# Memory V turned by transposing DMA instead of by the TensorE, at new places, with a branch hint for the sync engine

## The chip, the cores and the metric

The kernel runs on one NeuronCore of a Trainium2 chip. The metric is the device time of one execution in microseconds (us); the tables give the median of all runs of a kernel. "Granted clock" is the share of its full clock that the TensorE was allowed, as the profile gives it.

## The reference, cut to what matters

Two layers are computed side by side and concatenated. A is a complex diagonal recurrence over 2048 steps. B is attention in 64 segments of 32 tokens, each with 8 memory rows in front; the memory of the next segment is the output of the first 8 rows of this one.

```python
def _B_ref(x, mem0, Wq, Wk, Wv, Wo, seg_len):        # 32 heads of 128, model width 1024
    ...
    for s in range(n_seg):
        xs = x[:, s * seg_len:(s + 1) * seg_len, :].copy()
        h = jnp.concatenate([mem, xs], axis=1)
        q, k, v = (jnp.einsum('btd,dhe->bhte', h, W) for W in (Wq, Wk, Wv))   # three lines in the original
        scores = jnp.einsum('bhqe,bhke->bhqk', q, k) * scale
        ...
        o = jnp.einsum('bhqk,bhke->bhqe', softmax(scores), v)                 # two lines in the original
        o = jnp.einsum('bhte,hed->btd', o, Wo)
        mem = o[:, :M, :].copy()
        outs.append(o[:, M:, :])
```

What matters here is V of the 73 memory rows (`NM` = 7 + 66). It is made on the TensorE in eight blocks of four heads ("blocks 0 to 7"), comes out with the head dimension on the partitions, and must be turned so that the rows are on the partitions.

## The kernel before: the parts that the change touches

The kernel has four phases: projections of x, the recurrence (second phase, to about 471 us), the attention by head pairs `hp` = 0 to 15 (third phase), and the output projection. A scheduler orders the instructions of each engine, so program order is only a starting point, except where the code asks for it to be kept.

```python
def stage_init(self):                        # two staging buffers, used in turn
    self.vst = []
    for i in range(2):
        self.vst.append(self.wl.tile([128, 4, 4, EW], BF16, name=f"b_vst{i}", bufs=1))
        self.k.G.memset(self.vst[i][:, :, :, E:EW], 1.0)      # columns of ones, E = 128, EW = 136
    self.nst = 0

def next_st(self):
    self.nst += 1
    return self.vst[self.nst % 2]

def v_mem(self, hb, w=None):                 # block hb of memory V
    k = self.k
    w = w or self.load_wv(hb)
    p = k.ps("P")
    for h in range(4):
        for c in range(KC):
            k.PE.matmul(p[:, h * NM:(h + 1) * NM], w[:, c, h * 128:(h + 1) * 128], self.memT[:, c, :], ...)
    vm = self.vmp.tile([128, 4, NM], BF16, name="b_vm", bufs=1)
    k.copy("v", vm[:], p[:, 0:4 * NM].rearrange("p (h n) -> p h n", h=4))
    yield
    pt = k.ps("P", (128, 1024), BF16)
    for h in range(4):
        k.PE.transpose(pt[0:NM, h * 128:(h + 1) * 128], vm[:, h, :], k.ident[:])
    st = self.next_st()
    k.copy("v", st[0:NM, 0, :, 0:E], pt[0:NM, 0:512].rearrange("p (h e) -> p h e", h=4))
    sv = st[:, 0, :, :].rearrange("p h e -> p (h e)")
    k.SP.dma_start(self.vx[hb][64:64 + NMX, :], sv[0:NMX, :])      # 7 rows
    k.SP.dma_start(self.vt[hb][:], sv[NMX:NM, :])                  # 66 rows
    yield
...
def load_v(self, hp):                        # V of a head pair, for the attention
    vt = self.vts[hp % 2]
    if hp < 2:                               # fill rows 99 to 127 once in each of two buffers: 29 rows
        z = self.vx[0][T + 32:T + 32 + 128 - GW, 0:2 * EW].unsqueeze(1).to_broadcast([128 - GW, NG, 2 * EW])
        k.tc.keep_in_program_order(k.SP.dma_start(vt[GW:128, :, :], z))
    ...                                      # 96 rows from vx, 3 rows from vt
...
def hint(k):                                 # the branch over the rarely needed general path, near the end
    k.tc.mark_branch_hint_location("general", "LikelyTaken", engines=[mybir.EngineType.PE])
    i = k.nc.cur_bb.bb.instructions[-1]
    k.tc.keep_in_program_order(type("Ins", (), {"ins": i}))
...
# second phase, 30 steps i of the recurrence
    if i in (26, 28):
        vm = b.v_mem((i - 26) // 2, wv[(i - 26) // 2])
    if 26 <= i < 30:
        next(vm)
...
# third phase, 11 steps u of each head pair hp
    if n == 12:
        k.SP.dma_start(wo0[:], b.Wo[:, :, 0:512])              # 4 MB
    if hp % 2 == 0 and 2 < hp + 2 < HP:
        if u == 4:
            vm = b.v_mem(hp // 2 + 1)
        if u in (4, 6):
            next(vm)
```

SyncE issues nearly all DMAs (371 of 452 in the trace before), one after the other; a DMA that has to wait holds up those behind it (before, the load of `b_v` from `b_vx` at 466.40 us held SyncE for 16.05 us, and the load behind it went out at 482.50). A DMA has "landed" when its data have arrived and its semaphore says so.

## Time and profile before

| | before |
|---|---|
| median of 3 runs | 1246.7 us (1246.66 to 1246.81) |
| profiled span, granted clock | 1245.3 us, 0.999 |
| TensorE (PE) busy | 1234.2 us, 99% |
| last matmul ends, then to the end of the span | 1239.3 us, 6.0 us |

The page of the kernel before, its first, second and fourth part. In the second part every digit is the busy share, or the granted clock, of one fortieth of the span in tenths. In all views PE is the TensorE, PEld its loads of weights, DVE the VectorE, ACT the ScalarE, POOL the GpSimd engine, SP or SPq the SyncE; names that begin with ps are tiles in PSUM, the memory that the TensorE writes to.

```profile
span 1245.3 us, 20124 instructions
PE 1234.2 (99%) x8270; PEld 662.5 (53%) x8342; DVE 667.7 (54%) x1250; ACT 263.4 (21%) x631; POOL 275.8 (22%) x407
PE   9999999999999999999999999999999999999998
PEclk9999999999999999999999999999999999999999
PE 99%; issue 0%; DVE 0%
```

The TensorE is the bound everywhere. The list of waits of the TensorE over the whole run (engine, line, releaser: total us, times, longest) has one line, at the very start:

```profile
PE psR L64 <- DVE hpb L105: 1.3, 1, 1.3
```

The list of waits of SyncE's queue in the last 45 us shows, beside waits for the data of output stores, one long wait of its own after the closing branch (line L1156):

```profile
SPq L1156 <- SPq L1156: 2.8, 1, 2.8
```

SyncE's timeline around the first V load (start, us taken, engine, operation, out<-in). The V stores take 0.3 us each, and the loads of V follow directly. The last line holds two DMAs: issuing the 29 filler rows takes 0.32 us, and the 96 rows behind them hold SyncE for 16.05 us.

```profile
465.02 0.27 SPq L64 DMA_DIRECT2D b_vx<-b_vst  x1
465.34 0.29 SPq L64 DMA_DIRECT2D b_vt<-b_vst  x1
465.73 0.26 SPq L64 DMA_DIRECT2D b_v<-b_vt  x1
466.03 16.42 SPq L64 DMA_DIRECT2D b_v<-b_vx  x2
```

### The profile page before, as it was taken

The page shows a single profiled execution, that of the slowest core. Times are in us where ns is not written, and L with a number is a line of the kernel's source. Part 1 is how long each engine was busy: PE and PEld are TensorE (multiplying, and loading weights), DVE is VectorE, ACT ScalarE, POOL GpSimd, SP SyncE. Part 2 cuts the span into 40 slices and gives each one's busy share as a digit, 9 for nine tenths or more (in the row PEclk, how much of TensorE's full clock was granted, in tenths as well). Part 3 has the DMA queues.
Part 4 walks back from the last instruction along what each step waited for, and adds up shares of the span by engine and source line. Part 5 has one row for each costly group of instructions (what it writes and reads, how often), then busy time and mean ns, then how long its engine had stood idle before and what let it go on. Part 6 is the DMA issues. An engine that isn't in the chain of part 4 may idle for free.

```text
span 1245.3 us, 20124 instructions
## 1 busy us (share of the span) xinstructions
PE 1234.2 (99%) x8270; PEld 662.5 (53%) x8342; DVE 667.7 (54%) x1250; ACT 263.4 (21%) x631; POOL 275.8 (22%) x407
## 2 busy tenths in 40 slices
PE   9999999999999999999999999999999999999998
PEld 5444444444455555556666656555665554446444
DVE  4688899998711124666666666666666641001000
ACT  5344444443310000211112111111211110000000
POOL 4111331212332321322222222222222220000000
PEclk9999999999999999999999999999999999999999
DMA  9965444554898734664454545545553379407000
GB/s 248 272 191 147 131 135 127 144 155 107 242 322 248 249 116 95 196 170 124 96 145 108 144 108 120 132 92 121 120 142 92 65 211 230 107 18 153 17 26 19
DMA packets 316246, 176.83 MB, mean 142 GB/s; under 512 B 138874, under 2 KB 301550, under 8 KB 316150
## 3 DMA queue, kind: packets, MB, share of 16 engines
q1 hardware_dynamic: 294054, 147.95, 47.8%
q10 hardware_dynamic: 21072, 24.38, 5.9%
q0 software_dynamic: 1024, 3.17, 0.7%
q8 instruction: 66, 1.08, 0.4%
q14 instruction: 30, 0.25, 0.1%
HBM read 89.14 MB, written 53.17 MB: 114 GB/s over the span
## 4 chain that ended last, share of the span: by engine, by line
PE 99%; issue 0%; DVE 0%
PE psP L64 82%; PE psU L64 9%; PE psS L64 3%; PE psO L64 2%; PE psR L64 2%; DVE b_xe L91 0%; DVE b_ost L91 0%; DVE a_n L962 0%; DVE hpb L105 0%; DVE ones L102 0%
## 5 line engine op out<-in xcount | busy, mean ns | idle before, releaser
L64 PE MATMUL psP<-b_xe,b_wq 128*128 128x480 bf16 (+1 forms) x1280 | 247.7, 343 | 0.1
L64 PE MATMUL psP<-b_xe,b_wk 128*128 128x480 bf16 (+1 forms) x1280 | 247.7, 343 | 0.0
L64 PE MATMUL psP<-b_wv,b_xe 128*128 128x512 bf16 (+2 forms) x1033 | 223.4, 372 | 0.8
L644 POOL TENSOR_TENSOR b_m<-b_e,maskB 99x396 bf16<-99x396 bf16 x160 | 139.8, 874 | 338.5 <-ACT b_e L641 338.5
L641 ACT ACTIVATE b_e<-psS 99x396 bf16<-99x396 f32 x176 | 88.2, 501 | 536.7 <-PE psS L64 533.4
L64 PEld LDWEIGHTS <-b_wk 128*128 128x128 bf16 x1280 | 119.4, 98 | 94.2
L64 PEld LDWEIGHTS <-b_wq 128*128 128x128 bf16 x1280 | 118.7, 98 | 87.7
L64 PEld LDWEIGHTS <-b_xe 128*128 128x128 bf16 x1056 | 101.8, 98 | 119.1 <-DVE b_xe L91 0.2
L91 DVE CAST b_k<-psP 128x480 bf16<-128x480 f32 (+1 forms) x192 | 97.4, 528 | 100.9 <-PE psP L64 100.9
L91 DVE CAST b_q<-psP 128x480 bf16<-128x480 f32 (+1 forms) x192 | 97.4, 528 | 93.1 <-PE psP L64 91.5
L64 PEld LDWEIGHTS <-b_ol 128*128 128x128 bf16 x864 | 84.3, 98 | 94.4
L64 PE MATMUL psU<-a_xT,a_bt 128*128 128x512 bf16 x493 | 113.9, 379 | 1.1
L64 PE MATMUL psP<-t,a_hl 128*128 128x512 bf16 x496 | 112.1, 379 | 0.8
L91 DVE CAST b_ost<-psP 128x512 bf16<-128x512 f32 (+1 forms) x17 | 11.5, 676 | 177.4 <-PE psP L64 176.3
L64 PE MATMUL psP<-wo,b_ol 128*128 128x512 bf16 (+1 forms) x440 | 91.9, 364 | 0.4
L64 PE MATMUL psP<-t,b_ol 128*128 128x512 bf16 x408 | 91.7, 379 | 0.4
L280 POOL TENSOR_SCALAR a_tt<-a_pr,a_tabf 128x1 f32<-128x1 f32 x48 | 34.1, 710 | 243.2 <-DVE a_pr L275 243.2
L661 DVE TENSOR_TENSOR b_ob<-psO,b_accR 99x384 bf16<-99x384 f32 x160 | 85.9, 553 | 2.4 <-DVE b_accR L660 0.4
L89 ACT ACTIVATE b_vst<-psP 128x512 bf16<-128x512 f32 x126 | 71.9, 589 | 71.3 <-PE psP L64 59.9
L267 DVE TENSOR_TENSOR a_pr<-psU,a_tabf 128x2048 f32<-128x2048 f32 x32 | 73.0, 2282 | 15.7 <-PE psU L64 14.0
L64 PEld LDWEIGHTS <-a_bt 128*128 128x128 bf16 x512 | 49.2, 98 | 57.6
L64 PEld LDWEIGHTS <-a_hl 128*128 128x128 bf16 x512 | 49.0, 98 | 56.7
(200 smaller groups left out, 962.7 us busy)
## 6 DMA issues: line engine op xcount, KB each, us to landing
b_v<-b_vx SPq DMA_DIRECT2D x16, 1122.0 KB
b_wv<-in_B_Wv_dram SPq DMA_DIRECT2D x16, 1024.0 KB
b_vx<-b_vst ACTq DMA_DIRECT2D x24, 544.0 KB
b_on<-b_ob SPq DMA_DIRECT2D x15, 720.0 KB
a_hs<-a_h SPq DMA_DIRECT2D x32, 256.0 KB
b_wog<-in_B_Wo_dram SPq DMA_DIRECT2D x4, 2048.0 KB
b_wq<-in_B_Wq_dram SPq DMA_DIRECT2D x16, 512.0 KB
b_wk<-in_B_Wk_dram SPq DMA_DIRECT2D x16, 512.0 KB
```

Of the source, the lines that this page charges most:

```text
L64: r = f(*a, **kw)
L89: self.S.activation(out, in_, ACT.Copy)
L91: self.V.tensor_copy(out, in_)
L267: V.tensor_tensor(pr[:], u[:].unsqueeze(1).to_broadcast([128, 2, 2, TB]), view(t3, [[TB + 1, 2], [TB + 1, 2], [1, TB]]), ALU.mult)
L280: G.tensor_scalar(tt[:, j:j + 1], w[:, j, TB - 1:TB], t3[:, 1, TB:TB + 1], None, ALU.mult)
L641: k.S.activation(e[:], s[0:GW, :, :, 0:GW], ACT.Exp, scale=float(E) ** -0.5, accum_out=self.accE[0:GW, i:i + 1])
L644: k.G.tensor_tensor(m[0:GW, 0:4 * GP].rearrange("p (a b q) -> p a b q", a=2, b=2)[:, :, :, 0:GW], e[:], mask[0:GW, :, :].unsqueeze(2).to_b ...
L661: V.tensor_tensor(self.ob[:, b0:b0 + n, :], o[0:GW, 0:n, 0:E], r.unsqueeze(2).to_broadcast([GW, n, E]), ALU.mult)
```

## The change

The intent is threefold: take 32 transposes (four per block) from the TensorE and let DMA turn the blocks on a way through memory; move block 0 one step earlier and block 1 into the third phase, to make time for that longer way; and give SyncE the branch hint that the TensorE already has, so that its closing waits begin earlier. The staging buffer gets a new layout (stride 144), so its columns of ones have to be written anew.

```diff
+        self.vmt = [k.drp.tile([4, E, 128], BF16, name=f"b_vmt{i}") for i in range(HB)]
...
-        vm = self.vmp.tile([128, 4, NM], BF16, name="b_vm", bufs=1)
-        k.copy("v", vm[:], p[:, 0:4 * NM].rearrange("p (h n) -> p h n", h=4))
+        if hb == 0:
+            self.vm = self.vmp.tile([128, 4, 128], BF16, name="b_vm", bufs=1)
+            k.V.memset(self.vm[:, :, NM:128], 0.0)
+        k.copy("v", self.vm[:, :, 0:NM], p[:, 0:4 * NM].rearrange("p (h n) -> p h n", h=4))
+        k.SP.dma_start(self.vmt[hb].rearrange("h e n -> e h n"), self.vm[:])
         yield
-        pt = k.ps("P", (128, 1024), BF16)
+        s = self.next_st()[:].rearrange("p i h e -> p (i h e)")[:, 0:576].rearrange("p (h e) -> p h e", h=4)
+        k.V.memset(s[:, :, E:EW], 1.0)
         for h in range(4):
-            k.PE.transpose(pt[0:NM, h * 128:(h + 1) * 128], vm[:, h, :], k.ident[:])
-        st = self.next_st()
-        k.copy("v", st[0:NM, 0, :, 0:E], pt[0:NM, 0:512].rearrange("p (h e) -> p h e", h=4))
-        sv = st[:, 0, :, :].rearrange("p h e -> p (h e)")
-        k.SP.dma_start(self.vx[hb][64:64 + NMX, :], sv[0:NMX, :])
-        k.SP.dma_start(self.vt[hb][:], sv[NMX:NM, :])
+            k.SP.dma_start_transpose(s[:, h, 0:E], self.vmt[hb][h])
+        yield
+        k.SP.dma_start(self.vx[hb][64:64 + NMX, :].rearrange("n (h e) -> n h e", h=4), s[0:NMX, :, 0:EW])
+        k.SP.dma_start(self.vt[hb].rearrange("n (h e) -> n h e", h=4), s[NMX:NM, :, 0:EW])
         yield
...                                          # hint()
-    k.tc.mark_branch_hint_location("general", "LikelyTaken", engines=[mybir.EngineType.PE])
-    i = k.nc.cur_bb.bb.instructions[-1]
-    k.tc.keep_in_program_order(type("Ins", (), {"ins": i}))
+    for e in (mybir.EngineType.PE, mybir.EngineType.SP):
+        k.tc.mark_branch_hint_location("general", "LikelyTaken", engines=[e])
+        i = k.nc.cur_bb.bb.instructions[-1]
+        k.tc.keep_in_program_order(type("Ins", (), {"ins": i}))
...                                          # second phase
-                if i in (26, 28):
-                    vm = b.v_mem((i - 26) // 2, wv[(i - 26) // 2])
-                if 26 <= i < 30:
+                if i == 25:
+                    vm = b.v_mem(0, wv[0])
+                if 25 <= i < 28:
                     next(vm)
...                                          # third phase
-            if hp % 2 == 0 and 2 < hp + 2 < HP:
+            if hp % 2 == 0 and hp + 2 < HP:
                 if u == 4:
-                    vm = b.v_mem(hp // 2 + 1)
-                if u in (4, 6):
+                    vm = b.v_mem(hp // 2 + 1, wv[1] if hp == 0 else None)
+                if u in (4, 6, 8):
                     next(vm)
```

## The prediction

> **What bounds it now.** TensorE: the page's first part has PE busy 1234.2 of 1245.3 us, the chain of waits gives PE 99%, and the list of waits has one for PE, 1.3 us at the start. Only fewer PE slots, or a shorter start or end, can shorten the run. At the end, the last matmul finishes near 1239.3 us. SyncE issues the last output store at 1239.77, and its branch over the rarely taken general path starts at 1240.14; its next instruction, the first closing semaphore wait, starts only at 1243.00.
>
> **Removed from PE.** Eight groups of four transposes. By start times in the timeline each holds PE for 56 ns, in both phases, with neighbours packed against them: 32 x 56 ns = 1.79 us, all on the critical path. Eight VectorE copies (0.41 us each) go too (VectorE is 54% busy: worth nothing).
>
> **Added.** Per head block: a 128 KB store to memory, four transposing DMAs of 128x128, a small VectorE memset, and V stores cut into 272-byte rows instead of 1088. SyncE must wait for the store before the transposes, and for those before the V stores. In the trace a transpose of eight such blocks takes SyncE 1.3 to 1.5 us when the queue is free; my estimate from that is under 2 us of issue and 5 to 8 us of latency per head block.
>
> **Is that hidden?** I think so. For the first head pair, V's load starts now at 465.7, after both halves of the memory work; its first use on PE is at 492.2. With only the first block in the second phase, one step earlier, I estimate it starts near 458 to 462, so this deadline eases. The second block now sits beside the 4 MB load of Wo (issued at 517.2, moving until about 531), so its transposes may land near 530. The V load that depends on them went out at 532.95 for a use at 558.4 and took about 7 us: some 15 us of slack.
>
> **The hint.** [...] two 8 KB transfers on the instruction queue start at 1241.34, 1.2 us after SyncE's branch. If the hint brings the target in earlier, the closing waits begin at about 1240.5 and are held by the last output store, which lands from 1241.19 to 1241.49. The wait for it now passes at 1243.55, so the ceiling of the gain is 2.0 us. I give 75% that it works: PE, which has the hint already, ran its next instruction 1.1 us after its branch, at the end of its matmuls, which does not prove it.
>
> **Prediction.** 1246.7 - 1.8 - 1.9 = 1243.0 us, range 1242.3 to 1245.2. Faster by over 2%: 0.01; within 2%: 0.98; slower: 0.01.
>
> **What would show it.** 32 PE matmuls fewer and 1.8 us less busy time; still only the one PE wait; SyncE's first closing wait within 1 us of its branch and the last one at the landing of the last store; span after the last matmul from 6.0 to about 4 us.
>
> **What would make it wrong.** The hint does nothing (about 1244.9). Or SyncE, held in order by the new landings, issues loads so late that PE waits at a head boundary (near 492, 525 or 558 us): PE waits on b_v or b_wq would lose the gain.

## The result, and the profile after

| | before | after |
|---|---|---|
| median (4 runs each, same chip) | 1246.76 us (1246.66 to 1247.15) | 1264.25 us (1263.85 to 1264.58) |
| profiled span, granted clock | 1245.3 us, 0.999 | 1262.4 us, 0.994 |
| last matmul ends | 1239.28 us | 1258.62 us |
| from there to the end of the span | 5.98 us | 3.79 us |

The ratio is 1.014 (95% interval 1.0122 to 1.0157). Ratios are computed as the mean time of one kernel's fast runs over that of the other's of the same rounds, so they are not quite the ratio of the medians quoted. The change cost 17.5 us, 1.4%, where a gain of 3.7 us had been predicted.

The page after. The chain of waits now holds DMA, and three slices of the TensorE's row, at a bit under half of the run, are no longer full. The counts of matmuls (8270 and 8310) do not show the transposes saved, since 72 records are missing from the trace before; the weight loads do, 8342 and 8310: 32 fewer.

```profile
span 1262.4 us, 20198 instructions
PE 1237.8 (98%) x8310; PEld 660.9 (52%) x8310; DVE 666.6 (53%) x1251; ACT 263.4 (21%) x631; POOL 275.7 (22%) x407
PE   9999999999999998779999999999999999999998
PEclk9999999999999999989999999999999999999999
PE 94%; DMA 4%; SPq 1%; DVE 0%; issue 0%; ACT 0%; DVEq 0%; ACTq 0%
```

The waits of the TensorE after, whole run: four are new.

```profile
PE psP L64 <- DVE b_q L91: 15.2, 1, 15.2
PE psO L64 <- DMA b_v<-b_vx: 3.3, 1, 3.3
PE psR L64 <- DVE hpb L105: 1.3, 1, 1.3
PE psP L64 <- DMA b_wv<-in_B_Wv_dram: 0.6, 1, 0.6
PE psU L64 <- DMA b_xr<-in_B_x_dram: 0.4, 1, 0.4
```

Where the time went can be summed from the start times of certain matmuls in the two traces:

| stretch of the TensorE's work | before | after | difference | made of |
|---|---|---|---|---|
| start to first matmul of the recurrence | 347.52 | 348.38 | +0.86 | first loads end 0.6 to 1.1 us later |
| to the first Wq matmul of the third phase | 123.39 | 121.85 | -1.54 | 8 transposes fewer (-0.45), block 1's matmuls moved away (-1.09) |
| to the first matmul that uses V | 21.25 | 24.58 | +3.33 | wait for V |
| to the third head pair | 60.41 | 78.45 | +18.04 | wait 15.20, block 1's matmuls (+1.09), the rest (1.75) half clock after the wait |
| to the last matmul | 686.71 | 685.35 | -1.36 | 6 x 4 transposes fewer |
| to the end | 5.98 | 3.79 | -2.19 | SyncE after its branch |
| sum | | | +17.14 | the spans differ by 17.1 |

The second row is split with the help of e5 below, which turns both blocks by DMA at the old places: there this stretch is 0.45 us shorter than before.

So the TensorE did get its 1.8 us, the end of the run became 2.2 us shorter, and both were buried under two waits. The first question is the 15.2 us. Timeline of the TensorE around it: the last column is the idle time in front and what ended it. The eight matmuls after the wait take 3.36 us, twice the 1.78 us of eight alike ones before.

```profile
527.23 1.78 PE L64 MATMUL psP<-b_xe,b_wk 128*128 128x480 bf16 x8
529.02 0.50 PE L64 MATMUL psO<-b_v,b_m 128*128 128x129 bf16 x6
544.73 3.36 PE L64 MATMUL psP<-b_xe,b_wk 128*128 128x480 bf16 x8 [15.20 <-DVE b_q L91]
```

The TensorE waited for a VectorE cast that frees a tile in PSUM (`DVE b_q L91` in the line above). So look at what the VectorE did:

```profile
524.16 1.02 DVE L664 TENSOR_TENSOR b_ob<-psO,b_accR 99x384 bf16<-99x384 f32 x2
544.02 0.09 DVE L555 MEMSET b_vst<- 128x32 bf16 x1 [18.84 <-DMA b_vt<-b_vst]
544.02 0.65 DVE L91 CAST b_q<-psP 128x480 bf16<-128x480 f32 x1
```

It stood idle for 18.84 us in front of a memset of 0.09 us: the ones of the staging buffer. The memset waited for a store out of that buffer, block 1's V store, and a cast whose data had long been there stood behind it. The order of the program, engine by engine, says which memset it is: block 3's, which shares its buffer with block 1. The scheduler had moved it 181 instructions of the VectorE ahead of block 3's own copy out of PSUM, into the time when block 1 was still on its way.

SyncE's timeline after shows why that store was late. Block 1's way begins with the store at 516.52 and ends with the store at 539.42, which landed at about 543.9:

```profile
516.52 0.41 SPq L64 DMA_DIRECT2D b_vmt<-b_vm  x1
517.03 0.68 SPq L64 DMA_DIRECT2D b_wq<-in_B_Wq_dram  x1
517.76 1.62 SPq L64 DMA_DIRECT2D t<-in_B_Wo_dram  x1
519.47 10.27 SPq L64 DMA_DIRECT2D b_wk<-in_B_Wk_dram  x1
529.84 7.38 SPq L64 DMA_TRANSPOSE b_vst<-b_vmt  x4
538.52 0.86 SPq L64 DMA_DIRECT2D b_vx<-b_vst  x1
539.42 0.84 SPq L64 DMA_DIRECT2D b_vt<-b_vst  x1
```

Block 1's data had been ready since about 502.5, when the VectorE had copied them out of PSUM. SyncE could not issue the store before 516.52, because it was held by the V load of the second head pair, which has 29 filler rows of its own:

```profile
491.63 19.09 SPq L64 DMA_DIRECT2D b_v<-b_vx  x2
```

And this is block 0's way, to be set against the four lines of before. The four transposes take 1.15 to 1.23 us of SyncE each, the stores in short rows 0.98 and 0.84 us instead of 0.27 and 0.29. The first load of V goes out at 467.22, 1.5 us later than before although the block began a step earlier. The 17.12 us of the last line are again almost all spent on the 96 rows behind the filler rows.

```profile
450.21 0.63 SPq L64 DMA_DIRECT2D b_vmt<-b_vm  x1
455.86 4.98 SPq L64 DMA_TRANSPOSE b_vst<-b_vmt  x4
463.57 0.98 SPq L64 DMA_DIRECT2D b_vx<-b_vst  x1
464.59 0.84 SPq L64 DMA_DIRECT2D b_vt<-b_vst  x1
467.22 0.29 SPq L64 DMA_DIRECT2D b_v<-b_vt  x1
467.56 17.12 SPq L64 DMA_DIRECT2D b_v<-b_vx  x2
```

The clock: windows of 20 us after (busy us of each engine with the number of instructions, granted clock, DMA share, GB/s). The clock is at half from about 534 to 548 us (granted 0.50 in the windows 536 to 540, 540 to 544 and 544 to 547 us); most of that falls into the wait, so only the first 3.2 us of work pay for it.

```profile
520.00:540.00 20.00, 9.53 (x68) 5.22 (x66) 3.56 (x9) 2.36 (x8) 3.49 (x4) 0.86 0.88 266
540.00:560.00 20.00, 15.28 (x110) 9.30 (x110) 11.40 (x33) 2.36 (x8) 3.50 (x4) 0.80 0.86 222
```

At the end, SyncE's own waits behind its branch (two now) have shrunk from 2.8 to 0.7 us in sum, the longest 0.5:

```profile
SPq L1160 <- SPq L1160: 0.7, 2, 0.5
```

### The profile page after: what moved, and what is told of

It reads as the page before. It is cut to its first block, busy times and chain, and to the rows that moved or that the text cites. A ratio compares the mean times of both kernels' runs of the same rounds, so it can differ in the third digit from the quotient of the medians.

```text
span 1262.4 us, 20198 instructions
## 1 busy us (share of the span) xinstructions
PE 1237.8 (98%) x8310; PEld 660.9 (52%) x8310; DVE 666.6 (53%) x1251; ACT 263.4 (21%) x631; POOL 275.7 (22%) x407
## 4 chain that ended last, share of the span: by engine, by line
PE 94%; DMA 4%; SPq 1%; DVE 0%; issue 0%; ACT 0%; DVEq 0%; ACTq 0%
PE psP L64 78%; PE psU L64 9%; PE psS L64 3%; PE psO L64 2%; DMA b_v<-b_vx 2%; PE psR L64 2%; SPq L64 1%; DMA b_vt<-b_vst 1%; DMA b_wv<-in_B_Wv_dram 1%; DMA b_vst<-b_vmt 0%; DMA b_vmt<-b_vm 0%; ACT b_e L644 0%; DVE b_q L91 0%; DVE b_vm L91 0%; DVE b_ost L91 0%
## 5 line engine op out<-in xcount | busy, mean ns | idle before, releaser
L64 PE MATMUL psP<-b_xe,b_wk 128*128 128x480 bf16 (+1 forms) x1280 | 249.3, 344 | 15.2 <-DVE b_q L91 15.2
L91 DVE CAST b_k<-psP 128x480 bf16<-128x480 f32 (+1 forms) x192 | 97.5, 529 | 100.5 <-PE psP L64 100.5
L91 DVE CAST b_q<-psP 128x480 bf16<-128x480 f32 (+1 forms) x192 | 97.5, 529 | 91.9 <-PE psP L64 90.4
L91 DVE CAST b_ost<-psP 128x512 bf16<-128x512 f32 (+1 forms) x17 | 11.5, 676 | 177.4 <-PE psP L64 177.4
```

The lines of the kernel that those rows point to most:

```text
L64: r = f(*a, **kw)
L91: self.V.tensor_copy(out, in_)
```

## The experiments

**Theory A**: the 15.2 us come from the position of the ones-memset in the VectorE's order. It stands ahead of casts that the TensorE needs, and waits for the previous store out of the same buffer. **Rival B**: the late DMA itself, or the crowd on SyncE's queue with the 4 MB of Wo in it, holds the TensorE up. A third question is what shortened the end: the hint, or something else. Each group of runs was made on one chip with its own runs of the kernel before; before had medians of 1247.01, 1246.90 and 1247.14 us in the three groups. All kernels gave correct results.

### e1_hint_only: before, with the hint alone

```diff
-    k.tc.mark_branch_hint_location("general", "LikelyTaken", engines=[mybir.EngineType.PE])
-    ...
+    for e in (mybir.EngineType.PE, mybir.EngineType.SP):
+        k.tc.mark_branch_hint_location("general", "LikelyTaken", engines=[e])
+        ...
```

> The kernel before with the hint of the sync engine and nothing else. Theory: the hint by itself is worth the 2.2 us by which the end after the last matmul shrank in the changed kernel (5.98 to 3.79 us), so 1246.7 - 2.2 = 1244.5 us (1244.2 to 1244.9), SyncE's gap between its branch and its first closing wait about 0.5 us instead of 2.8, nothing else moved. Rival: the shorter end of the changed kernel came from something else [...]; then the hint alone gives 1246.7 and the gap stays 2.8.

Measured: 1247.04 us, ratio 1.0001 (0.9984 to 1.0017). The expectation failed. The hint instruction is in the trace at 1212.79, 27.5 us ahead of the branch. No 8 KB instruction fetch follows it before 1241.24, behind the branch, and the wait is unchanged; SyncE's waits in the last 45 us:

```profile
SPq L1157 <- SPq L1157: 2.7, 1, 2.7
```

So the hint alone, at this place, gains nothing, and the 2.2 us must come from something else in the change.

### e2_ones_twice: after, ones written for the first two blocks only

Later blocks find the ones already in the buffer, since nothing else overwrites these columns.

```diff
-        k.V.memset(s[:, :, E:EW], 1.0)
+        if hb < 2:
+            k.V.memset(s[:, :, E:EW], 1.0)
```

> The changed kernel with the ones columns set only for the first two head blocks, so once for each of the two staging buffers (right result: nothing overwrites them later). Same order of DMA issues on SyncE. Theory A (VectorE in order): the 15.2 us wait of PE at 529 us is VectorE standing at the memset of the fourth block, which waits for the V store of the second; without it that wait is gone and with it the slow matmuls after it: 1264.2 - 15.2 - 1.7 to 2.5 = 1246.5 to 1247.5 us, the 3.3 us wait on b_v near 491 remains, the V store of the second block still lands near 544. Theory B (the loads that PE needs are late because SyncE and the DMA queues are jammed by the transposes and the 4 MB load): PE then waits at 530 to 560 for operands instead, and the time stays above 1258.

Measured: 1247.14 us, ratio 1.0006 (0.9989 to 1.0022). The 15.2 us wait and the half clock are gone (granted clock 1.00 in all windows from 491 to 560 us). The TensorE's waits from 480 to 600 us:

```profile
PE psO L64 <- DMA b_v<-b_vx: 2.8, 1, 2.8
```

Block 1's V store was issued at 538.72 us, only 0.7 us earlier than after, and hurt nobody. This fits A and speaks against B, but the edit also takes away six VectorE instructions; e12 below closes that gap.

### e3_wo_late: after, the 4 MB load of Wo one head pair later

```diff
-            if n == 12:
-                k.SP.dma_start(wo0[:], b.Wo[:, :, 0:512])
+            if n == 24:
+                tc.keep_in_program_order(k.SP.dma_start(wo0[:], b.Wo[:, :, 0:512]))
```

> The changed kernel, memsets as they are, with the 4 MB load of half of Wo kept in program order one head pair later, so that it is no longer in front of the second block's transposes. Theory A: the V store of the second block lands earlier (near 531 instead of 544), VectorE's wait at the memset shrinks with it to 5 to 9 us and PE's to 3 to 7 us: 1251 to 1256 us. If the lateness of the store came from the transposes themselves (1.2 us of SyncE each) and not from the 4 MB load, the store still lands near 540 and the time stays near 1262 to 1264.

Measured: 1264.63 us, ratio 1.0141 (1.0124 to 1.0158). The expectation failed. Without Wo in between, block 1's way was quicker (Wk's issue took 1.19 us instead of 10.27) and its store landed at 534.3, about 10 us earlier. But the scheduler had placed the memset 13 VectorE instructions earlier as well, and the V load of the first pair was later. The waits of the VectorE and of the TensorE from 480 to 600 us:

```profile
DVE b_vst L555 <- DMA b_vt<-b_vst: 15.9, 1, 15.9
PE psP L64 <- DVE b_k L91: 12.4, 1, 12.4
PE psO L64 <- DMA b_v<-b_vx: 4.5, 1, 4.5
```

Both waits came with a lower clock here (granted 0.83 from 490 to 500 us, 0.51 from 530 to 540 us). Wo made the store 10 us late, and removing 10 us of lateness did not remove the stop: from the store of the block (517.62) to the landing of its V (534.3) the way takes 16.7 us even without Wo.

### e4_places_only: before, with the new places of the blocks alone

The diff is that of the last two parts of the change, with turning on the TensorE (two steps per block), and no hint.

> The kernel before, turning by TensorE, without the hint, with only the places moved: first block one step earlier in the second phase, second block in the third. Theory: the places alone cost nothing and gain nothing, since TensorE has the same work and V's first load goes out earlier: 1246.4 to 1247.2 us, no PE wait above 1 us. Rival (the move of the second block into the third phase, beside the load of Wo, is what hurts): over 1250 us with a wait of PE or VectorE near 520 to 545.

Measured: 1246.71 us, ratio 0.9998 (0.9982 to 1.0015). As expected, the places alone cost and gain nothing.

### e8_ones_twice_no_hint: e2 without the hint

The edit is that of e2, and `hint()` as before.

> The kernel with the ones written for the first two blocks only (e2, 1247.14 us), with the sync engine's hint taken out again. Theory 'place in the program': the 2.2 us shorter end comes from where the sync engine's closing branch falls among the blocks in which its instructions are fetched, and the hint does nothing: the time stays at 1247.1 +- 0.5 and the gap from the sync engine's branch to its first closing wait stays near 0.55 us. Theory 'hint': the time rises by 2.2 us to 1249.3 +- 0.5, and the gap is 2.8 us again.

Measured: 1247.15 us (1246.03 to 1248.22), ratio 1.0004 (0.9987 to 1.0021), gap 0.53 us. The end stays short without the hint. The runs scatter by 2.2 us, more than those of most other kernels: two with a granted clock of 0.999 and 1.000 took 1246.55 and 1246.03 us, two with 0.998 took 1248.22 and 1247.76 (e2 is alike: 1246.6 us at 0.999 and 1.000, 1247.6 and 1248.7 at 0.998). The likely reason, an estimate, is that the wait for V is sometimes followed by a spell of lower clock and sometimes not (from 491 to 500 us the granted clock is 0.81 in e12, with a wait of 2.5 us, and 1.00 in e2, with one of 2.8 us); the slower runs have no trace. So the time alone would not decide it; the gap in the trace does.

### e9_before_40_drains: before, with 40 do-nothing instructions on SyncE

Counted in the trace, SyncE's closing branch is its instruction 588 in before and 642 after. Every kernel with the branch beyond 600 shows an 8 KB instruction fetch just as SyncE reaches its instruction 592 to 595, 70 to 200 us ahead of the end; the kernels with the branch at 588 or 589 do not, they fetch 1.0 to 1.2 us behind the branch. After has a fetch there too, at 1260.67, 1.2 us behind its branch, but its first closing wait had already started at 1260.04; before, the fetches start at 1241.34 and the first closing wait at 1243.00. If that is all, moving the branch past that place is enough.

```diff
         for n, (hp, u) in enumerate(at):
+            if n == 100:
+                for _ in range(40):
+                    tc.keep_in_program_order(nc.sync.drain(fusable=False))
```

> The kernel before, no hint, with 40 instructions that do nothing (drains) on the sync engine in the middle of the third phase, where it has time to spare, so that its closing branch is instruction 628 and no longer 588. Theory 'place in the program': the branch now falls past the block boundary at instruction 593, the gap from branch to first closing wait drops from 2.7 to about 0.55 us, and the time to 1244.7 +- 0.6. Theory 'hint': nothing changes, 1246.9 +- 0.5.

Measured: 1244.53 us (1244.36 to 1244.83), ratio 0.9982 (0.9965 to 0.9999). SyncE's waits in the last 45 us:

```profile
SPq L1159 <- SPq L1159: 0.7, 2, 0.5
```

A kernel that does nothing but waste 40 instructions is 2.4 us faster. The gap between branch and first closing wait in all kernels:

| kernels | SyncE's branch is its instruction | hint | gap, us |
|---|---|---|---|
| before, e4 | 588 | no | 2.86, 2.73 |
| e1 | 589 | yes | 2.77 |
| e5, e8, e9, e10 | 605 to 644 | no | 0.53 to 0.54 |
| after, e2, e3, e6, e7, e11, e12 | 630 to 650 | yes | 0.55 to 0.56 |

The hint makes no difference in either group; the place does.

### e10_store_only: before, with the new tensors and one store into each

This asks for the 0.86 us at the start, and is a second test of the place.

```diff
+        self.vmt = [k.drp.tile([4, E, 128], BF16, name=f"b_vmt{i}") for i in range(HB)]
...
         k.copy("v", vm[:], p[:, 0:4 * NM].rearrange("p (h n) -> p h n", h=4))
+        k.SP.dma_start(self.vmt[hb].rearrange("h e n -> e h n")[:, :, 0:NM], vm[:])
```

> The kernel before, PE turning as before, with the eight additional memory tensors of the change and a store of each block into its own that nobody reads. Asks for the 0.86 us that every kernel with these tensors lost before its first matmul of the recurrence (348.4 us against 347.5). If the tensors themselves cost it, the start is 348.4 here too; if it is something of the transposing DMAs, 347.5. It has 17 more instructions on the sync engine, so its closing branch is about number 605, past 593: theory 'place' says gap 0.55 us, theory 'hint' 2.7. Together: 1244.6 (place, tensors free), 1245.5 (place, tensors cost 0.86), 1247.8 (hint, tensors cost 0.86).

Measured: 1244.99 us (1244.52 to 1245.22), ratio 0.9984 (0.9968 to 1.0001), gap 0.53 us with the branch at 605. The first matmul of the recurrence starts at 347.58 us, so tensors and stores do not cost the start.

### e7_first_by_pe: after, with block 0 turned by the TensorE, ones written once into each buffer

```diff
+        if hb == 0:
+            yield
+            ...                              # turning as in the kernel before
+            return
...
-        k.V.memset(s[:, :, E:EW], 1.0)
+        if hb in (1, 2):
+            k.V.memset(s[:, :, E:EW], 1.0)
...
-                if 25 <= i < 28:
+                if 25 <= i < 27:
                     next(vm)
```

> The changed kernel with block 0 of memory V still turned by the TensorE, blocks 1 to 7 by transposing DMA, and the ones written only once into each buffer. If the 2.8 us wait for block 0's V at the start of the third phase is due to the longer way by DMA, it goes: from e2's 1247.14 down by 2.8 and up by 0.22 for four turns on the TensorE to 1244.6 +- 0.7. If that wait has another cause (the different place of block 0, or the single-engine load of 29 rows), it stays and the time is 1247.4.

Measured: 1244.44 us (1244.31 to 1244.56), ratio 0.9981 (0.9964 to 0.9998). The TensorE's wait for V at the start of the third phase is gone, so the longer way of block 0 was needed for it.

### e12_ones_pinned: after, with every ones-memset held at its place in program order

```diff
-        k.V.memset(s[:, :, E:EW], 1.0)
+        k.tc.keep_in_program_order(k.V.memset(s[:, :, E:EW], 1.0))
```

> The changed kernel with one thing more: each of the eight writes of ones is held at its place in program order on the VectorE, so that the scheduler cannot move it forward. SyncE and TensorE have the very same instructions in the same order as the changed kernel; all eight writes, both buffers and the 19 us late store of block 1 remain. Theory A (a write of ones that stands too early in the VectorE's order holds up the casts behind it until block 1's store has landed): the 15.2 us wait and the half clock after it go, 1247.1 +- 0.7. Rival (the late store itself, or the SyncE, holds the TensorE up, or the additional VectorE work does): 1264 +- 1.

Measured: 1248.03 us (1247.77 to 1248.41), ratio 1.0008 (0.9992 to 1.0025): 0.23 us above the range that theory A expected and 16 us below that of the rival. The TensorE's program is the same as after, instruction for instruction. SyncE issues the same DMAs in the same order, but, unlike what was expected, with one more semaphore wait in front of each block's first V store (8 instructions more). On the VectorE everything but the memsets stands in the same order. Block 1's V store is issued at 538.25, as late as in e2. The VectorE now works straight through the time at which it stood still before:

```profile
526.14 0.66 DVE L91 CAST b_q<-psP 128x480 bf16<-128x480 f32 x1 [0.34 <-PE psP L64]
528.05 0.66 DVE L91 CAST b_q<-psP 128x480 bf16<-128x480 f32 x1 [0.72 <-PE psP L64]
```

This is the cleanest evidence for theory A: all eight memsets and the late store are still there, and the place of the memsets in the VectorE's order makes or removes the stop. The kernel is 0.9 us slower than e2, although it waits for V only 2.5 us. The clock says why: the window from 491 to 500 us, first of e12, then of e2 (same columns as above, clock third from the end), shows 0.81 against 1.00, worth 1.7 us. All four runs of e12 had a granted clock of 0.998, of e2's only the two slower ones.

```profile
491.00:500.00 9.00, 6.52 (x38) 3.40 (x37) 3.75 (x9) 1.18 (x4) 1.75 (x2) 0.81 0.42 103
```

```profile
491.00:500.00 9.00, 6.20 (x47) 3.46 (x46) 3.88 (x9) 1.18 (x4) 1.75 (x2) 1.00 0.50 114
```

### e6_pad32: e2, with the filler load as 32 rows instead of 29

After, the 29 rows go over about one DMA engine. In a stretch in which little but these rows moves (480 to 484 us), the core moves 21 GB/s, and the busy share of its 16 DMA engines is 0.07; from 471 to 480 us the 312 packets of their queue take 6.1% of the time of 16 engines, where one engine is 6.25%. That 32 rows spread wider is what the author expected of this run; why 29 do not was not shown. Rows 96 to 98, which the 32 rows also cover, are loaded with their own data behind it.

```diff
-                z = self.vx[0][T + 32:T + 32 + 128 - GW, 0:2 * EW].unsqueeze(1).to_broadcast([128 - GW, NG, 2 * EW])
-                k.tc.keep_in_program_order(k.SP.dma_start(vt[GW:128, :, :], z))
+                z = self.vx[0][T + 32:T + 64, 0:2 * EW].unsqueeze(1).to_broadcast([32, NG, 2 * EW])
+                k.tc.keep_in_program_order(k.SP.dma_start(vt[GX:128, :, :], z))
...
-                k.SP.dma_start(wo0[:], b.Wo[:, :, 0:512])
+                tc.keep_in_program_order(k.SP.dma_start(wo0[:], b.Wo[:, :, 0:512]))
```

> e2 (ones written for the first two blocks only, 1247.14 us), with the first of the loads of block 0's V for the attention made of 32 rows in place of 29, so that it spreads over more than one of the DMA engines, and the 4 MB load of Wo held in program order. If the 2.8 us wait for V at the start of the third phase is due to that load on a single engine, which took some 16 us ahead of the other rows, the wait goes: 1244.3 +- 0.7. If the longer way of block 0 (store, four turns, store) is the cause alone, it stays: 1247.1.

Measured: 1243.61 us (1243.51 to 1244.16), ratio 0.9973 (0.9956 to 0.9990). The wait for V is gone, and the two DMAs that took SyncE 17.12 us after take 1.15 us:

```profile
465.40 1.15 SPq L64 DMA_DIRECT2D b_v<-b_vx  x2
```

The load of Wo, which this edit also pins, goes out at 508.23, after the time of the wait, so it is not what removed it. In the trace, the last packet of the first V load now starts at 475.7 instead of 493.0 us (e2). From 465 to 475 us the core moves 85 to 313 GB/s, and the 374 KB of the 32 rows are through within 10.3 us, 36 GB/s or more, so they go over more than one engine.

The quicker load has a second effect, which the expectation did not name. Block 1's store no longer stands behind the filler rows of the second head pair and goes out 17 us earlier than in e2 (515.85):

```profile
498.80 0.39 SPq L64 DMA_DIRECT2D b_vmt<-b_vm  x1
```

So the filler rows had made block 1 late as well as Wo. Whether 32 rows alone, with the memsets left where the scheduler put them, would have avoided the 15.2 us stop was not run.

This is the fastest kernel, with all eight blocks turned by DMA. e6 and e7 together say that the wait for V needed both: the longer way of block 0 (e7 takes it away) and the single-engine load (e6 takes that away). The kernel before carries the second without harm, but only just: the last packet of its load starts at 491.22 and the first use is at 492.16, while after it starts at 493.34.

### e11_third_phase_only: blocks 0 and 1 by the TensorE at the old places, the rest by DMA

```diff
+        if hb < 2:
+            yield
+            ...                              # turning as in the kernel before
+            return
...
+        if hb in (2, 3):
+            k.V.memset(s[:, :, E:EW], 1.0)
...                                          # places of blocks 0 and 1 as before; hint and the rest as in the change
```

> A version meant to beat both: blocks 0 and 1 turned by the TensorE at their old places in the second phase, blocks 2 to 7 by transposing DMA in the third, ones written once into each buffer, hint as in the change. No wait for V at the start of the third phase, no stop of the VectorE. Sum: 1246.9, less 6 x 0.224 = 1.34 us of TensorE, less 2.2 us at the end (the sync engine's branch comes past instruction 593), plus 0.9 us at the start if that belongs to transposing DMA: 1244.4 +- 0.7. If the start costs nothing here: 1243.4.

Measured: 1244.68 us (1244.53 to 1245.01), ratio 0.9981 (0.9965 to 0.9998), as expected with the late start, and no faster than e7. The first matmul of the recurrence starts at 348.16 us, so the late start is there although no block is turned by DMA before the third phase.

### e5_method_only: turning by DMA at the old places, no hint, ones as in e2

```diff
-                if i == 25:
-                    vm = b.v_mem(0, wv[0])
-                if 25 <= i < 28:
+                if i in (26, 28):
+                    vm = b.v_mem((i - 26) // 2, wv[(i - 26) // 2])
+                    next(vm)
+                if i in (27, 29):
+                    next(vm)
                     next(vm)
...                                          # third phase: blocks 2 to 7, as before
```

> Only the method of the change, with the blocks at the old places (blocks 0 and 1 late in the second phase), no sync hint, and ones written for the first two blocks only. Block 0's way through memory and the single-engine load of 29 rows start about 4 us later than in the change, and block 1's turn stands in the sync engine's order ahead of the load of V. So the wait for V at the start of the third phase should grow from 2.8 to some 7 to 14 us, with the clock halved for a few us after it: 1257 +- 5, worth telling what the new places buy. If the places are not what matters, 1247.

Measured: 1259.72 us (1259.38 to 1260.44), ratio 1.0103 (1.0086 to 1.0120). The TensorE's waits from 480 to 600 us:

```profile
PE psO L64 <- DMA b_v<-b_vx: 13.6, 1, 13.6
```

The load of V goes out at 479.43, behind both blocks' ways. So the new places, which gain nothing by themselves (e4), are worth some 11 us of waiting once the blocks go by DMA.

## Why the prediction was wrong, point by point

- **What bounds the kernel: right.** The TensorE, at 99%. The 18.5 us of new waits (15.2 and 3.3) show in full in the two stretches that hold them (+18.04 and +3.33 us).
- **The TensorE's 1.8 us: right, to the size.** Six blocks gave -1.36 us in the stretch to the last matmul, blocks 0 and 1 together -0.45 us (e5).
- **The failed step is "Is that hidden?".** It has two parts.
  - A block was put at under 2 us of issue and 5 to 8 us of latency. Its way measured 17.0 us for block 0 (store at 450.2, V load at 467.2), 16.7 us for block 1 without Wo (e3), and 27.4 us after (516.5 to 543.9). The issue seems to have been scaled by size from DMAs of eight 128x128 blocks (1.3 to 1.5 us each), but a DMA of one block takes SyncE 1.15 to 1.23 us too, so four took 4.98 us; the V stores took 1.8 us more. The rest of block 0's way is three landings in a row that SyncE has to sit out, of which the first alone took 5.6 us, with a 1 MB load issued just ahead of it. So the first deadline did not "ease" to 458 to 462 us: the load went out at 467.2 and cost 3.3 us. That is a wait on b_v, a risk that the prediction had named. The single-engine load behind it, which already stood in the old trace as a 16.4 us issue, left no room (e6): it ended some 1 us before the first use of V already before the change.
  - The second block's transposes landed near 538 rather than "near 530", and that would still have met its V load: e2 and e12 have the same late store and no wait for it. The prediction asked who needs the block's data, and not who waits for the buffer. It called the memset "a small VectorE memset" and costed its duration, 0.09 us. The memset is also a write into a shared buffer, so it waited for the store two blocks back, and the scheduler had moved it far forward. The VectorE stood idle in front of it for 18.84 us, and a cast whose data had been there since about 527.4 us ran only behind it, at 544.02. This wait, the 15.2 us, the prediction did not foresee. The reordered program was there to be read before the run.
- **The clock was not in the sum.** The 15.2 us wait cost about 1.75 us more in half-clock matmuls (eight that take 1.78 us took 3.36). Waits of 15.2 us (after, granted 0.50 from 536 to 547 us), 13.6 us (e5, 0.995 over the run, 0.999 in before), 12.4 and 4.5 us (e3, 0.51 from 530 to 540 and 0.83 from 490 to 500 us) came with a lower clock, waits of 3.3 us (after, 1.00 from 491 to 500 us) and 2.8 us (e2, 1.00) did not, and one of 2.5 us did (e12, 0.81). So the length of a wait alone does not decide it here; what else does was not shown.
- **The hint: right in size by luck, wrong in cause.** The end became 2.2 us shorter for a predicted 1.9. But e1 shows that the hint gains nothing (1247.04 us against 1247.01), e8 that the gain stays without it (gap 0.53 us), and e9 that 40 wasted instructions alone bring it (1244.53 us against 1246.90). That the branch of before waits for a fetch is not shown, though the trace fits it: two 8 KB fetches start 1.2 us behind the branch, and the next instruction 1.7 us behind them. That the hint would bring the closing waits forward was the author's estimate, and e1 failed it. The 54 additional SyncE instructions of the change moved the branch from instruction 588 to 642, beyond the fetch at 592 to 595. That this fetch had brought the target in is an inference from the fetch times; that the place decides is shown (gap 0.53 to 0.56 us against 2.73 to 2.86).
- **The start: not foreseen, and open.** All kernels that turn blocks by DMA start the recurrence at 348.1 to 348.4 us, against 347.5 in before and 347.2 to 347.6 in those that do not. It is neither the tensors nor the stores (e10) nor the early blocks (e11). In the trace the first loads, in the same order, take longer per packet (31.3 to 31.6 ns instead of 27.0 for the first 512-byte packets, in exactly the kernels that start late). Why is not settled.

The sum with what was measured: 1246.8 - 1.8 (TensorE) - 2.2 (end) + 0.9 (start) + 3.3 (wait for V) + 15.2 (stopped VectorE) + 1.75 (clock) = 1264.0 us, for 1264.25 measured.

## What to carry to other kernels

When work moves from a saturated engine to DMA, cost the whole way as a chain of landings, and then list every instruction that touches the buffers of that way: here a memset of 0.09 us that waited for a store held up the VectorE for 18.84 us and the casts behind it with it, and the scheduler had moved it to that place. Either write constants such as ones only once per buffer or hold such an instruction at its place, and compare the order of each engine before and after. Before crediting a gain to one part of a change, run that part alone: here a 2.2 us gain came from where a branch happened to fall, and 29 rows against 32 decided another wait.
